# Block-causal attention with a gated MLP on one core: the value product of one pair moved directly ahead of the next pair's scores

## The chip, the core and the metric

The kernel runs on one core of one Trainium2 chip. The metric is the device time of one execution in microseconds (us). The kernel before the change has a median of 1179.65 us over three runs (1178.62 to 1180.1). PE is the matrix engine (TensorE), PEld its weight loads, DVE is VectorE, ACT is ScalarE, POOL is GpSimd, and SP is SyncE, whose queue issues most of the DMAs.

## What is computed

The reference, cut to what matters:

```python
# q, k, v: (B=8, H=8, S=576, D=64); block = 64
scores = (q @ k.T) / sqrt(D), masked to block_i >= block_j
attn   = exp(scores - max); attn = attn / (attn.sum(-1) + 1e-9)
x      = (attn @ v).transpose(0, 2, 1, 3).reshape(4608, 512)
gate   = 1 / (1 + exp(-(x @ w_gate)));  val = x @ w_val     # 512 -> 1536
out    = (gate * val) @ w_out                               # 1536 -> 512
```

Everything is float32 at the ends. Inside, many matrix products are made of three products of high and low parts (`H*H + H*L + L*H`), whose operands carry the letters H and L in the profile.

## The kernel before, in words

**Stages.** The 64 heads are taken as 32 pairs, four pairs for each of the 8 batches. A loop over `p` from 0 to 32 (lines 812 to 856) works on pair `p` and finishes pair `p-1` in the same turn. The first third of the MLP's hidden columns (`F1` = 4 blocks of 128) for batch `b` is computed while the attention of later batches runs; its matrix products are the filler between the attention's steps. After the loop the rest of that filler is run (lines 986 and 987), and then comes a second phase over the remaining hidden columns (`unit` and `out_block`, lines 887 to 977), which this change does not touch.

**One pair.** With rows of scores in 128-blocks `i` = 0 to 3 and a last block of 64 rows for both heads together (the tail):

- `s_blocks` (step `s`, line 393) makes the scores of blocks 3, 2 and (1, 0), each group in a PSUM tile of two banks. The two heads lie on partitions 0 to 63 and 64 to 127, and each has its own half of PE's rows (`tile_position=(64 * h, 0)`, line 377), so that two products run side by side. DVE writes the mask (lines 409, 411) and takes the row maximum (line 385), ACT takes exponentials into the tiles `P` (line 388).
- `s_tail` (step `t`, line 415) makes the tail's scores with the whole height of PE, six products of 288 columns; ACT writes the tile `Pt` (line 427).
- `tr_main(3)`, `tr_main(2)`, `tr_low`, `tr_tail` (steps `tr3`, `tr2`, `trl`, `trt`) transpose the exponentials on PE (line 262), and ACT copies them out of PSUM into `G1` and `G0` (line 363). The tail's copies go into columns of `G1` (line 485).
- `recip` (step `r`, line 430) turns the row sums into reciprocals, writes them to DRAM (`r_d`, line 439) and reads them back broadcast (`rb`, line 442), over SP's queue.
- `av` (step `AV`, line 493) multiplies with the values, 28 products in 14 side-by-side couples, where each head has its own half of PE's columns (`tile_position=(0, 64 * h)`, line 501). DVE multiplies the result by `rb` into `xT` (line 507). Then `finish` (line 512) casts `xT` on ACT, sends it to DRAM on ACT's queue and subtracts on POOL.
- `prep(p+1)` (steps `k` and `q`) transposes the next pair's K and Q on DVE (line 290), splits them on ACT, DVE and POOL (lines 327 to 336).

PE thus has three ways to be cut: the whole array (MLP products, the tail's scores, the transposes), two halves of rows (scores) and two halves of columns (AV).

**The order of the steps** stands in tuples of (step, places). `ALONE`, `FIRST` and `TURN` serve pairs 0 to 7, `REST` pairs 8 to 31. A place is a point behind a step at which MLP products are dealt out (lines 836 to 851): `rate` products for each place, which is 3.0 from pair 12 on, thus 36 for the 12 places of a pair. Step names in `REST` that begin with `AV` belong to pair `p-1`, the others to pair `p`. When the AV of a batch's last pair has been written down, the MLP products of that batch are added to those left, and `rate` is set anew so that 32 remain over when the next batch comes (lines 821 to 825). `k`, `q` and `r` have no place.

**What fixes the order on PE.** The program is scheduled by a list scheduler which simulates the engines; `behind(a, b)` (line 70) adds an edge that keeps `a` behind `b` without a semaphore. In the steps of `REST`:

- `hold` is the last matrix product of the latest scores or AV (lines 402 and 504). Every transpose and every product dealt out later stands behind it (lines 263, 845).
- `dealt` is the last MLP product dealt out. The first product of the scores (line 401) and of the AV (line 503) stands behind it.
- A product that is dealt out also stands behind the attention's step of three places earlier (`AHEAD` = 3, lines 847 and 848), so it may run up to three places early where the attention's step is not ready.

**PSUM.** The scores, the AV and the transposes of `REST` take their two-bank tiles (`two_banks`, line 267) from one rotation of three, in the order in which the steps are written down; MLP products use two further single banks (`mbank`).

Of the kernel before, what the change touches and what calls it, by code (L numbers as in the profile page):

```python
# [21 lines left out]
AHEAD = 3  # L22
# [8 lines left out]
         ("tr3", 1), ("r", 0), ("ld", 0))  # L31
ALONE = (("S3", 1), ("TR2", 1), ("k", 1), ("S2", 1), ("q", 1), ("m3", 0), ("m2", 0), ("TRt", 1), ("t", 1), ("TRl", 1), ("sl", 1), ("AV", 2),
         ("tr3", 1), ("r", 0), ("ld", 0))
REST = (("s", 3), ("t", 1), ("AV", 2), ("tr3", 1), ("r", 0), ("k", 0), ("tr2", 1), ("q", 0), ("trl", 2), ("trt", 2))
TURN = (("s3", 1), ("TR2", 1), ("k", 0), ("s2", 1), ("TRt", 1), ("q", 0), ("t", 1), ("TRl", 1), ("sl", 1), ("AV", 1),
        ("tr3", 1), ("r", 0), ("tr2", 1), ("trl", 1), ("trt", 1))
N_FIRST = 7
# [5 lines left out]
def attn_glu_kernel(ctx: ExitStack, tc: tile.TileContext, q, k, v, w_gate, w_val, w_out, out):  # L43
# [26 lines left out]
    def behind(ins, other):  # L70

        tc.add_manual_dep(ins, other.name, mybir.DependencyInfo(mybir.DependencyClass.NoSync,
                                                                mybir.DependencyReason.DATA), reason="order")
# [84 lines left out]
    def run(gen):  # L158
        for _ in gen:
            pass  # L160
# [3 lines left out]
    with ExitStack() as s2:  # L164
# [78 lines left out]
        pe_last, first_mm, hold, dealt, chain = [], [], [], [], []  # L243
# [23 lines left out]
        def two_banks():  # L267
            return ps_a.tile([P, 2, 512], F32, name="bank")
# [80 lines left out]
        def attend(p):  # L349
# [10 lines left out]
            rest = p > N_FIRST  # L360
# [4 lines left out]
            def scores(ps, i, c):  # L365


                n = P * (i + 1)
                q = slice(i * P, (i + 1) * P)
                ops = [(KQ[:, 1, q], KQ[:, 0, :n])]  # L370
                if rest and i:
                    q = slice((i - 1) * P, i * P)
                    ops = [(QS[a][:, q], KS[b][:, :n]) for a, b in ((0, 0), (1, 0), (0, 1))]
                for k, (x, y) in enumerate(ops):
                    for h in range(2):
                        matmul(ps[:, h, c:c + n], lhsT=x[rows(h)], rhs=y[rows(h)], start=(k == 0),
                               stop=(k == len(ops) - 1), tile_position=(64 * h, 0))
                        if h == k == 0:
                            first_mm[:] = pe_last

            def softmax(ps, i, c):
                n = P * (i + 1)
                c0 = col[i]
                Pi = keep[i] = p_tile(i)
                mark("DVE", nc.vector.tensor_reduce(out=nm[:, c0:c0 + 2], in_=ps[:, :, c:c + n], axis=AX.X, op=ALU.max,  # L385
                                                    negate=True))
                for h in range(2):
                    mark("ACT", nc.scalar.activation(out=Pi[:, h], in_=ps[:, h, c:c + n], func=AF.Exp,  # L388
                                                     bias=nm[:, c0 + h:c0 + h + 1], accum_out=sm[:, 5 * h + i:5 * h + i + 1]))
                    if i == 3 and 0 < p < NP:  # L390
                        behind(last["ACT"], q_copied[-1])

            def s_blocks(*groups, alone=False):


                tiles = [two_banks() for _ in groups]
                for k, (ps, group) in enumerate(zip(tiles, groups)):
                    for j, i in enumerate(group):
                        scores(ps, i, 2 * P * j)
                        if rest and dealt and k == j == 0:  # L400
                            behind(first_mm[0], dealt[-1])
                if rest:
                    hold[:] = pe_last
                if alone:
                    yield
                for ps, group in zip(tiles, groups):
                    n = P * (group[0] + 1)
                    if len(group) == 1:
                        nc.vector.memset(ps[0:64, :, n - 64:n], -1e9)  # L409
                    else:  # L410
                        nc.vector.memset(ps[0:64, :, P:3 * P].rearrange("p h (i n) -> p h i n", i=2)[:, :, :, 64:], -1e9)
                    for j, i in enumerate(group):
                        softmax(ps, i, 2 * P * j)
# [109 lines left out]
            def step(what):  # L523
                if what in ("S3", "S2"):
                    soft[what] = s_blocks((int(what[1]),), alone=True)
                    next(soft[what])
                elif what in ("m3", "m2"):
                    run(soft.pop("S" + what[1]))
                elif what == "s":
                    run(s_blocks((3,), (2,), (1, 0)))  # L530
                elif what[0] == "s":
                    run(s_blocks({"s3": (3,), "s2": (2,), "sl": (1, 0)}[what]))
                elif what == "t":
                    s_tail()
                elif what == "r":
                    recip()
                elif what == "tr3":
                    tr_main(3)
                elif what == "tr2":
                    tr_main(2)  # L540
                elif what == "trl":
                    tr_low()
                elif what == "trt":
                    tr_tail()
                else:
                    av()
                    finish()
# [243 lines left out]
        pe_ticks = []  # L791

        def convert_to(p, part):
            for j, plan in enumerate(CONV_PLAN):
                convert_until(j, sum(plan[i] for i in plan if i < p) + int(plan.get(p, 0) * part))
# [3 lines left out]
        def early_work(p, tick):  # L799

            when = p - (n - 1), tick
            if when in ((0, 0), (1, 0)):
                early.append(fetch_gv(0, 0, 0, len(early)))
                early_x.append(x_load(0, len(early_x)))
            if when == (0, TICKS - 2):
                sums_gv(*early[0], alone=last["DVE"])
            if when == (1, 1):
                x_sums(early_x[0], nc.vector, last["DVE"])
            if when == (1, 4):
                sums_gv(*early[1], alone=last["DVE"])  # L810

        for p in range(n + 1):
            early_work(p, 0)
            pr = prep(p + 1) if p + 1 < n else iter(())
            now = attend(p) if p < n else None
            tick = 0
            for what, places in (ALONE if p < NP else FIRST if p < N_FIRST else TURN if p == N_FIRST else REST):
                if what.startswith(("AV", "TR")):
                    if prev:
                        prev(what.lower() if what == "AV" else what.lower()[:2] + what[2:])  # L820
                    if prev and what == "AV" and pairs[p - 1][1] == NP - 1:
                        pb = pairs[p - 1][0]
                        mlp = itertools.chain(mlp, mlp1(pb, mbank if p < n else bank))
                        left += F1 * 6 * NC + 3 * F1 * 4
                        rate = (left - KEEP[pb > 0]) / (4 * TICKS)
                elif what in "kq":
                    next(pr, None)
                    if p >= NP and p + 3 < n:
                        load(p + 3, what)
                elif what == "ld":  # L830
                    if p < NP:
                        for x in "kq":
                            load(p + 3, x)
                elif now:
                    now(what)
                for _ in range(places if now else 6 if what == "AV" else 0):
                    pe_ticks.append(pe_last[0])
                    acc += rate
                    while acc >= 1:
                        acc -= 1  # L840
                        left -= 1
                        ins = next(mlp, None)
                        if ins is not None:
                            dealt[:] = [ins]
                            if hold:
                                behind(ins, hold[0])
                            if len(pe_ticks) > AHEAD:
                                behind(ins, pe_ticks[-1 - AHEAD])
                    tick += 1
                    convert_to(p, min(1.0, tick / (TICKS - 2)))  # L850
                    early_work(p, tick)
            convert_to(p, 1.0)
            run(pr)
            if 0 < p and p + 2 < n:
                load(p + 2, "v")
            prev = now
# [238 lines left out]
```

## Time and profile before

| | |
|---|---|
| median of three runs | 1179.65 us (1178.62 to 1180.1) |
| profiled execution, from its first to its last instruction (span) | 1177.6 us |
| DVE, ACT, POOL busy | 776.6, 617.4, 349.6 us |
| weight loads busy | 976.3 us |
| MLP products of 512 columns from `XH` on tile `m`, mean | 0.400 us |
| transposes of 128 columns on tile `bank`, mean | 0.273 us |

The profiled execution is listed with its span alone; what lies around the span is taken from the difference to the runs, 2.05 us to their median.

How to read it: a matrix product's row gives its modelled duration, which is longer than the distance to the next product, since products are pipelined. What a product costs is therefore read from the start of one row to the start of the next. In a timeline, neighbouring instructions of a kind are one row with a count (`x2` for the two halves side by side). The chain of work that ended last is listed as start, length and what ran. In a view by windows, each engine has its busy time in that stretch and its number of instructions in brackets.

### The profile page before, as it was taken

What the parts mean: (1) busy time and instruction counts of PE and PEld (TensorE: products, weight loads), DVE (VectorE), ACT (ScalarE), POOL (GpSimd) and SP (SyncE); (2) the same over time, 40 slices, a digit from 0 to 9 for tenths busy, and PEclk for the clock granted to TensorE, in tenths of its full rate; (3) what the DMA queues carried; (4) which work ended last, traced back from release to release, by engine and by line L of the source; (5) the groups of instructions that cost most, each with busy time, mean ns of one, the idle gap of its engine ahead of it and who ended that gap; (6) DMA issues with size and microseconds to landing.
All of it is one profiled execution on the core that took longest, in us unless ns stands there. A gap on an engine that the chain in (4) does not pass through costs nothing.

```text
span 1177.6 us, 19283 instructions
## 1 busy us (share of the span) xinstructions
PE 1153.6 (98%) x6749; PEld 976.3 (83%) x6749; DVE 776.6 (66%) x1405; ACT 617.4 (52%) x1364; POOL 349.6 (30%) x390
## 2 busy tenths in 40 slices
PE   6999999999999999999999999999999999999998
PEld 4555778778777877787889899999999998998997
DVE  5778845454564555457959977867877746746754
ACT  5867766766676676666334443553453422423421
POOL 2345523222331322234002133032033263262330
PEclk8999999999999999999999999999999999999999
DMA  8765434435434443534323236235197455164241
GB/s 198 180 144 115 104 89 100 117 74 127 99 89 112 102 122 71 125 105 134 111 95 126 91 120 223 71 136 202 39 339 276 158 172 179 39 212 132 83 143 54
DMA packets 253361, 153.34 MB, mean 130 GB/s; under 512 B 193232, under 2 KB 215248, under 8 KB 252624
## 3 DMA queue, kind: packets, MB, share of 16 engines
q1 hardware_dynamic: 241600, 132.15, 40.1%
q10 hardware_dynamic: 11280, 18.91, 4.4%
q8 instruction: 53, 0.87, 0.3%
q0 software_dynamic: 384, 1.05, 0.3%
q14 instruction: 44, 0.36, 0.1%
HBM read 104.73 MB, written 47.33 MB: 129 GB/s over the span
## 4 chain that ended last, share of the span: by engine, by line
PE 90%; DVE 5%; ACT 2%; issue 1%; DMA 1%; POOL 0%; SPq 0%; DVEq 0%; ACTq 0%
PE b L875 27%; PE bank L258 14%; PE m L131 14%; PE m L953 11%; PE m L138 7%; PE bank L262 6%; PE b L953 5%; PE bank L131 3%; ACT P L388 1%; PE m L262 1%; PE bank L138 1%; DVE nm L385 1%; DVE XL L765 0%; DMA raw<-in_moe_w_out_dram 0%; DMA rqk<-in_k_dram 0%
## 5 line engine op out<-in xcount | busy, mean ns | idle before, releaser
L875 PE MATMUL b<-XH,w 128*128 128x384 f32 x1344 | 349.2, 335 | 1.2 <-DVE g L921 1.2
L875 PEld LDWEIGHTS b<-XH,w 128*128 128x128 f32 x1344 | 243.9, 188 | 5.2 <-DVE g L921 1.6
L875 PE MATMUL b<-XL,w 128*128 128x384 f32 x672 | 223.5, 335 | 0.0
L388 ACT ACTIVATE P<-bank,nm 128x512 f32<-128x512 f32 (+3 forms) x256 | 132.1, 530 | 68.3 <-DVE nm L385 68.2
L385 DVE TENSOR_REDUCE nm<-bank 128x2 f32<-128x1024 f32 (+3 forms) x128 | 105.4, 823 | 40.7 <-ACT P L388 37.6
L875 PEld LDWEIGHTS b<-XL,w 128*128 128x128 f32 x672 | 126.1, 188 | 1.6
L953 PE MATMUL m<-wo,hH 128*128 128x512 f32 x384 | 125.0, 391 | 0.0
L363 ACT COPY G<-bank 128x768 f32<-128x768 f32 (+3 forms) x140 | 93.2, 694 | 26.2 <-PE bank L262 25.3
L258 PE MATMUL bank<-G,VS 128*64 128x320 f32 (+4 forms) x896 | 93.9, 360 | 0.1
L751 POOL TENSOR_TENSOR XB<-XB 128x384 f32<-128x384 f32 x20 | 20.7, 1037 | 237.9 <-DMA XB<-xT_d 191.6
L138 PE MATMUL m<-wo,hH 128*128 128x512 f32 x256 | 85.4, 398 | 1.4 <-ACT ost L632 1.0
L258 PEld LDWEIGHTS bank<-G,VS 128*64 128x64 f32 x896 | 55.9, 137 | 36.7 <-issue 4.3
L900 ACT ACTIVATE g<-g 128x384 f32<-128x384 f32 x72 | 37.8, 526 | 88.5 <-DVE g L913 48.6
L953 PEld LDWEIGHTS m<-wo,hH 128*128 128x128 f32 x384 | 72.0, 188 | 13.5
L131 PE MATMUL m<-XH,wv 128*128 128x512 f32 x240 | 82.3, 400 | 0.0
L131 PE MATMUL m<-XH,wg 128*128 128x512 f32 x240 | 82.1, 399 | 0.0
L764 ACT CAST XH<-XB 128x1536 fp32r<-128x1536 f32 (+2 forms) x72 | 65.2, 941 | 29.4 <-DVE XB L762 24.1
L765 DVE TENSOR_TENSOR XL<-XB,XH 128x1536 fp32r<-128x1536 f32 (+2 forms) x72 | 75.8, 1084 | 0.0
L262 PEld LDWEIGHTS bank<-ident,P 128*128 128x128 f32 x560 | 65.8, 141 | 11.5 <-ACT P L388 0.8
L953 PE MATMUL m<-wo,hL 128*128 128x512 f32 x192 | 75.2, 392 | 0.0
L262 PE MATMUL bank<-ident,P 128*128 128x128 f32 x560 | 74.8, 273 | 0.1
L409 DVE MEMSET bank<- 64x128 f32 x64 | 10.6, 165 | 88.0 <-PE bank L258 87.3
(183 smaller groups left out, 2339.5 us busy)
## 6 DMA issues: line engine op xcount, KB each, us to landing
xT_d<-xT ACTq DMA_DIRECT2D x32, 288.0 KB
XB<-xT_d SPq DMA_DIRECT2D x16, 576.0 KB
part_d<-ost SPq DMA_DIRECT2D x36, 256.0 KB
VS<-in_v_dram SPq DMA_DIRECT2D x64, 128.0 KB
part_d<-ost ACTq DMA_DIRECT2D x32, 256.0 KB
rqk<-in_k_dram SPq DMA_DIRECT2D x108, 72.0 KB
rqk<-in_q_dram SPq DMA_DIRECT2D x108, 72.0 KB
wgv_d<-st SPq DMA_DIRECT2D x8, 896.0 KB
```

Source lines behind the costliest of these rows:

```text
L131: mm = nc.tensor.matmul(ps, lhsT=lh, rhs=rh, start=(i == 0), stop=(i == n - 1))
L138: mm = nc.tensor.matmul(ps, lhsT=lh[:, f, t * P:(t + 1) * P], rhs=rh, start=(f == i == 0), stop=(f == F1 - 1 and i == 2))
L258: pe_last[:] = [nc.tensor.matmul(*args, **kw).ins]
L262: pe_last[:] = [nc.tensor.transpose(*args).ins]
L363: mark("ACT", nc.scalar.copy(out=dst, in_=src))
L385: mark("DVE", nc.vector.tensor_reduce(out=nm[:, c0:c0 + 2], in_=ps[:, :, c:c + n], axis=AX.X, op=ALU.max, negate=True))
L388: mark("ACT", nc.scalar.activation(out=Pi[:, h], in_=ps[:, h, c:c + n], func=AF.Exp, bias=nm[:, c0 + h:c0 + h + 1], accum_out=sm[:, 5 * h ...
L764: nc.scalar.copy(out=XO[j][0][:, a:b], in_=x)
L765: sub = nc.vector.tensor_sub(out=XO[j][1][:, a:b], in0=x, in1=XO[j][0][:, a:b].bitcast(F32))
L875: mm = nc.tensor.matmul(ps, lhsT=lh, rhs=rh, start=(first and k == 0), stop=(k == n - 1), skip_group_check=not first)
L900: mark2("ACT", nc.scalar.activation(out=t, in_=c, func=AF.Tanh, scale=0.5))
L953: mm = nc.tensor.matmul(po[t], lhsT=lh[:, f, t * P:(t + 1) * P], rhs=rh, start=(half == 0 and i == 0), stop=(half == 1 and i == 5))
```

## The change

Three things are changed, all for pairs 8 to 31, with one side effect on pair 7.

- In `REST` the step `AV` (of pair `p-1`) moves from behind the tail's scores to the front, ahead of the scores of pair `p`, and has no place. Its two places go to `s` (3 becomes 4) and to `t` (1 becomes 2). A pair has 12 places as before.
- The first product of the scores now stands behind both the last MLP product dealt out and `hold`, which at that point is the AV's last product; so the scores follow the AV.
- An MLP product that is dealt out behind `trt` stands behind the tail's transposes themselves (`ahead_by` = 0 in place of `AHEAD` = 3). In `REST` these are two places, six products at a rate of 3.0. The AV, next in order, stands behind the last of them. The step `trt` of `TURN` (pair 7, one place) falls under the same rule.

```diff
-REST = (("s", 3), ("t", 1), ("AV", 2), ("tr3", 1), ("r", 0), ("k", 0), ("tr2", 1), ("q", 0), ("trl", 2), ("trt", 2))
+REST = (("AV", 0), ("s", 4), ("t", 2), ("tr3", 1), ("r", 0), ("k", 0), ("tr2", 1), ("q", 0), ("trl", 2), ("trt", 2))
...
                         scores(ps, i, 2 * P * j)
-                        if rest and dealt and k == j == 0:
-                            behind(first_mm[0], dealt[-1])
+                        if rest and k == j == 0:
+                            for ins in (*dealt, *hold):
+                                behind(first_mm[0], ins)
...
                             if hold:
                                 behind(ins, hold[0])
-                            if len(pe_ticks) > AHEAD:
-                                behind(ins, pe_ticks[-1 - AHEAD])
+                            ahead_by = 0 if what == "trt" else AHEAD
+                            if len(pe_ticks) > ahead_by:
+                                behind(ins, pe_ticks[-1 - ahead_by])
```

Since the AV of a batch's last pair now comes four places earlier in the turn, the products of that batch are added four places earlier too. Counted through the loop, 976 products have been dealt out by the end of pair 31 where 964 had been before; the total is the same.

## Prediction

> **What bounds the kernel now.** First the page: the busy times and the chain that ended last.
>
> ```profile
> PE 1153.6 (98%) x6749; PEld 976.3 (83%) x6749; DVE 776.6 (66%) x1405; ACT 617.4 (52%) x1364; POOL 349.6 (30%) x390
> PE 90%; DVE 5%; ACT 2%; issue 1%; DMA 1%; POOL 0%; SPq 0%; DVEq 0%; ACTq 0%
> ```
>
> PE carries the chain. Second the view by windows, for the stage that the change edits (most of pairs 9 to 31 with their MLP filler) and for the rest of the filler. The columns are window, its length, busy time of PE, PEld, DVE, ACT, POOL with instruction counts, and the granted clock.
>
> ```profile
> 188.97:546.00 357.03, 357.03 (x2442) 282.86 (x2443) 194.78 (x383) 240.80 (x599) 100.58 (x142) 1.00 0.44 104
> 546.00:615.00 69.00, 69.00 (x316) 56.30 (x313) 52.20 (x90) 26.91 (x40) 8.77 (x5) 1.00 0.36 114
> ```
>
> PE is not idle for one moment of the first 357 us, at full clock. In such a stage only two things can move the time: PE's own work becomes shorter, or PE is made to wait where it does not wait now. No product is added or removed here, so a gain has to come from what products cost by their order. Third, then, the chain in order of time through one pair (start, length, what, count):
>
> ```profile
> 356.88 2.00 PE bank L258 x21
> ...
> 361.85 3.65 PE bank L258 x34
> 365.49 1.58 PE m L131 x6
> ...
> 372.49 0.55 PE bank L262 x5
> 373.04 0.92 PE m L131 x4
> 373.96 2.00 PE bank L258 x21
> ```
>
> A pair takes 373.96 - 356.88 = 17.08 us. The 21 are the scores, the 34 the tail's scores (6) and the AV (28), the five the tail's transposes, with four MLP products between them and the next scores.
>
> **What a change of PE's cut costs.** Fourth, the timeline of PE around these places. `x2` is a couple side by side.
>
> ```profile
> 356.25 0.63 PE L138 MATMUL m<-wo,hH 128*128 128x512 f32 x2
> 356.81 0.50 PE L258 MATMUL bank<-KH,QH 64*128 64x512 f32 x2
> 357.14 0.39 PE L258 MATMUL bank<-KH,QL 64*128 64x512 f32 x2
> 357.38 0.40 PE L258 MATMUL bank<-KL,QH 64*128 64x512 f32 x2
> ...
> 362.21 0.29 PE L258 MATMUL bank<-KH,QBL 128*128 128x288 f32 x1
> 362.34 0.29 PE L258 MATMUL bank<-KL,QBH 128*128 128x288 f32 x1
> 362.56 0.49 PE L258 MATMUL bank<-G,VS 128*64 128x320 f32 x2
> ...
> 364.89 0.60 PE L258 MATMUL bank<-G,VS 128*64 128x256 f32 x6
> 365.42 0.50 PE L131 MATMUL m<-XL,wg 128*128 128x512 f32 x1
> 365.75 0.39 PE L131 MATMUL m<-XH,wg 128*128 128x512 f32 x1
> ```
>
> The mean of the AV's widest form is in the groups by form:
>
> ```profile
> L258 PE MATMUL bank<-G,VS 128*64 128x320 f32 x384 | 58.7, 441 | 0.1
> ```
>
> An MLP product in a row of such takes 0.92 / 4 = 0.23 us (the x4 row of the chain). Against that:
>
> - MLP to scores: two products take 356.81 - 356.25 = 0.56, so the second 0.33; the first couple of scores 0.33; the next one, of the same 512 columns, 0.24. Two steps, each 0.10 too long: 0.20 us.
> - Tail's scores to AV: the last product takes 0.22 where the one before took 0.13, 0.09 too long. The first AV couple has a duration of 0.49 where the mean of its form is 0.44, 0.05 too long (an estimate, durations being modelled): 0.14 us.
> - AV to MLP: the last three couples (256, 128 and 128 columns) take 0.53. The whole AV takes 365.42 - 362.56 = 2.86 us for 3200 columns (each product of values and probabilities is two instructions); with the long steps off, some 2.71, so 512 columns should take 0.43: 0.10 too long. The first MLP product takes 0.33: 0.10 too long. Together 0.20 us.
> - Scores to MLP is left as it is by the change, and cancels.
>
> So each change of cut costs 0.14 to 0.20 us, in two steps. Fifth, the two crossings that the new order needs and that appear early in the trace, scores to AV in pair 1 and MLP to AV in pair 8, with tail's scores to MLP ahead of the latter:
>
> ```profile
> 42.55 0.60 PE L258 MATMUL bank<-KQ 64*128 64x256 f32 x6
> 43.08 0.49 PE L258 MATMUL bank<-G,VS 128*64 128x320 f32 x2
> ...
> 170.75 0.29 PE L258 MATMUL bank<-KL,QBH 128*128 128x288 f32 x1
> 170.88 0.40 PE L131 MATMUL m<-XH,wg 128*128 128x512 f32 x1
> 171.21 0.49 PE L258 MATMUL bank<-G,VS 128*64 128x320 f32 x2
> ```
>
> From row halves to column halves, three couples of the same 512 columns take 0.53 again, 0.10 too long, and the first AV couple has the same 0.49: 0.15 us. Two tiled steps next to each other thus pay as much as a tiled one next to the whole array. MLP to AV: 0.33 for 0.23, plus 0.05: 0.15 us. Tail's scores to MLP: 0.13, the ordinary distance: nothing.
>
> **The sum.** Before, a pair crosses MLP to scores (0.20), scores to MLP, tail to AV (0.14), AV to MLP (0.20). After, it crosses MLP to AV (0.15), AV to scores, scores to MLP, and the tail's scores lie between MLP products at no cost. AV to scores is not in the trace. Its lower bound is nothing, the upper one a full AV to MLP and a full MLP to scores, 0.40. I take 0.20, by the nearest row, scores to AV, which pays one crossing and not two; the scores' own second step is 0.10, the AV's last 0.10. The gain of a pair is 0.20 + 0.14 + 0.20 - 0.15 - 0.20 = 0.19 us. Over 24 pairs that is 4.6 us (with AV to scores at nothing 9.4, at 0.40 nothing or 0.2 lost).
>
> [...]
>
> **What could wait.** The held products cost PE nothing (transposes to MLP is crossed once, as now). They are the cover for the copies out of the tail's transposes, which the AV needs at once now, where scores and tail's scores lay between before. ACT's rows, and DVE's ahead of the mask:
>
> ```profile
> 364.97:373.82 8.85, 5.57 (x10) 1.00 0.54 124
> ```
>
> ```profile
> 367.81 0.68 ACT L514 CAST XH<-xT 128x576 fp32r<-128x576 f32 x1
> ...
> 373.07 0.75 ACT L363 COPY G<-bank 128x512 f32<-128x512 f32 x2 [1.60 <-PE bank L262]
> ```
>
> ```profile
> 357.94 0.17 DVE L409 MEMSET bank<- 64x128 f32 x1 [5.99 <-PE bank L258]
> ```
>
> The copies end at 373.82, 0.78 us after the transposes (373.04). Six products cover 6 x 0.23 = 1.38: 0.60 us to spare if ACT takes the copies at once. Without cover each pair would lose the 0.78, 19 us in all.
>
> ACT's queue is in order. The first row is ACT from the end of the exponentials to the end of these copies: 5.57 busy of 8.85 us, among it 0.68 for the cast of `xT`. After the change the AV starts 17.08 - 0.19 - 2.87 (3.65 less the tail's six at 0.13) = 14.02 after the scores, that is 370.90 on this scale, so 5.93 us behind the exponentials. The cast moves to the free time ahead of the next exponentials, and 4.89 us remain for those 5.93. It fits, with 1.04 us for waits inside. So I cost the wait at nothing.
>
> DVE's multiplication into `xT` comes ahead of the softmax, in its idle 5.99 us. It holds one of the three PSUM tiles, which the last group of scores now needs, two groups (about 1.3 us) after the AV's end; the two multiplications take 0.8. SP's queue keeps its order behind pair `p`'s reciprocals, and the loads of `VS`, which wait for AV, come earlier:
>
> ```profile
> 368.22 1.74 SPq L442 DMA_DIRECT2D rb<-r_d  x3
> ```
>
> ```profile
> 46.89 1.98 DMA VS<-in_v_dram
> ```
>
> The three issues end at 369.96; with some 2 us to landing (an estimate from the second row, a DMA on the chain) `rb` is there at 371.9, 15.1 after its scores. The first multiplication wants the AV's 2432 first columns of 3200, about 2.1 us behind the AV's start, 16.1 after the scores: 1.0 to spare.
>
> Pair 7's tail transposes have two held products behind them instead of six. Cover 0.46 to 0.6 for 0.78 and a weight load: up to 0.4 us once. I take 0.4.
>
> **Behind the loop.** Twelve products (2.7 us) come ahead of the last AV instead of behind it. PE's total stays, but the DVE work that starts with the last AV has 2.7 us less of PE's time beside it until
>
> ```profile
> 597.80 0.69 DVE L150 SCALAR_TENSOR_TENSOR h<-t,bank 128x512 f32<-128x512 f32 x1 [1.78 <-PE bank L131]
> ```
>
> where DVE waits for PE, for the first time since its block began. Bounds 0 and 2.7 - 1.78 = 0.9 us if the order is kept, 2.7 at most. I take nothing, since products of the last batch can fill in. From there on PE leads, and all moves up together.
>
> Together 4.6 - 0.4 = 4.2 us: span 1177.6 - 4.2 = 1173.4. The median of before lies 2.05 us above the span, so 1175.4 us. About 0.2% (2.4 us) is what a measurement of this kernel can tell from no change.
>
> **Rivals.**
>
> 1. *Slower: the AV waits for the tail's copies.* If ACT's order puts two further steps of 0.6 us (a glu's cast and tanh) between the transposes and the copies, the copies end 1.2 later, 0.6 past the cover; 24 x 0.6 = 14.4, less 4.2: 1190 us. It decides from 0.19 us past the cover for each pair, that is, when the copies start 0.8 us or more behind the transposes. For it: ACT is 4.89 of 5.93 us full there. Against: the copies are ready ahead of what the held products set free. 0.13.
> 2. *Part of it is lost* to the same wait in some pairs, or behind the loop: 1 to 3.5 us lost, 1176.4 to 1178.9. 0.15.
> 3. *The price moves along.* If AV to scores pays leaving and entering in full, four steps of 0.10, 0.40 in all, the gain of a pair is nothing: 1179.65, with pair 7's 0.4 1180. Against it: every crossing in the trace has two long steps. It also covers the case that the scheduler keeps MLP products between AV and scores. 0.10. [...]
>
> [...]
>
> 4. *More:* AV to scores is nearly free: 24 x 0.39 - 0.4 = 9.0, 1170.7. Against: scores to AV is not free. 0.07.
>
> The forecast, a gain of 3.3 to 5.3, has 0.55.
>
> **Numbers.** The range 1172.5 to 1180.5 takes in the forecast, rivals 2 and 3 and a little of the others; outside lie most of 1 and 4, under 0.2. Faster by over 0.2% (under 1177.3): forecast, 4 and two thirds of 2 (0.10), 0.72. Same: rival 3 and the rest of 2, 0.15. Slower: rival 1, 0.13.
>
> **What would show it.** Right: pairs from 12 on take 16.9 us in the chain, PE is still busy in all of that stage, the AV and the 21 scores stand as one row of about 4.9 us, the step from the AV's last couples to the scores is 0.53 again, and six MLP products stand between the tail's transposes and the AV. Wrong: PE waits on ACT's copies (line 363) or DVE's `xT` (line 507) at the AV or the scores; an AV-to-scores step that is not 0.1 long; a stretch from 546 to 615 with PE idle.

## The result, and the profile after

The kernel after takes 1192.81 us (median of four runs, 1190.52 to 1194.33); the kernel before, on the same chip, 1179.24 (four runs, 1178.62 to 1180.1). The ratio is 1.0111, with a 95% interval of 1.0099 to 1.0123: slower by 13.6 us, where 4.2 us less was forecast. The profiled execution has a span of 1190.0 us against 1177.6. Among all the runs below, one execution, of run 3, took 5636 us; it is left out of that run's figures.

The page of the kernel after, its busy times and the chain that ended last (line numbers are one higher than before from line 402 on, two higher from 849 on):

```profile
PE 1154.5 (97%) x6749; PEld 978.9 (82%) x6749; DVE 777.9 (65%) x1405; ACT 616.6 (52%) x1364; POOL 344.6 (29%) x390
PE 80%; DVE 7%; DMA 5%; SPq 3%; issue 3%; ACT 2%; POOL 0%; DVEq 0%; ACTq 0%
```

PE does the same work in about the same busy time, but carries 80% of the chain instead of 90%. DMA, DVE and SP's queue have come in. PE's waits from 164 to 546 us (total, times, longest), a stretch in which it had none:

```profile
PE bank L258 <- DVE xT L508: 6.0, 7, 1.6
```

The instruction that waits is the first product of the scores of blocks (1, 0). It needs the PSUM tile that the AV has just filled, and DVE frees that tile with the multiply into `xT`. What that multiply waited for stands in the view of the tile `rb`, from 164 to 546 us: total idle time of DVE ahead of the multiply, and in how many pairs.

```profile
L508 DVE TENSOR_TENSOR xT<-bank,rb x43: 414/491/492, 173.8 to 545.9; 128x320 f32<-128x320 f32 x22, 128x256 f32<-128x256 f32 x21
its engine sat idle before it (us, times) until:
  DMA rb<-r_d: 51.2, 11
  DMA rqk<-in_k_dram: 24.8, 6
  PE bank L258: 19.3, 4
  DMA rqk<-in_q_dram: 6.4, 1
```

In 18 of 22 pairs a DMA ended DVE's idle time, by this view `rb` itself or a load on the same queue, and only in 4 it was the AV. The same view of the kernel before has no idle time ahead of the multiply at all. The chain in order of time, here through one of the worst pairs, reads as a loop from one pair's tail's scores to the next pair's scores:

```profile
420.71 4.79 PE m L138 x20
425.50 0.81 PE bank L258 x6
426.33 0.77 DVE nm L426
427.12 0.84 ACT Pt L428 x2
...
428.69 0.30 SPq L440
...
430.54 0.50 SPq L239
...
432.76 0.60 SPq L443
...
433.39 4.17 DMA rb<-r_d
...
437.69 0.10 DVE xT L508
...
438.66 0.85 PE bank L258 x10
```

Twenty MLP products, the tail's scores (x6), maximum, exponential, reciprocals, the write of `r_d`, two loads of K, the read of `rb`, the multiply, and then the ten products of scores that had to wait. The timeline of PE shows the wait itself:

```profile
432.67 2.93 PE L258 MATMUL bank<-G,VS 128*64 128x320 f32 x28
...
436.68 0.34 PE L258 MATMUL bank<-KL,QH 64*128 64x384 f32 x2
438.66 0.39 PE L258 MATMUL bank<-KH,QH 64*128 64x256 f32 x2 [1.64 <-DVE xT L508]
```

The worst place is pair 8, whose moved AV belongs to pair 7: PE's waits there are

```profile
127.03 2.93 PE L258 MATMUL bank<-G,VS 128*64 128x320 f32 x28 [1.86 <-ACT G L363]
135.32 0.39 PE L258 MATMUL bank<-KH,QH 64*128 64x256 f32 x2 [3.95 <-DVE xT L508]
```

What was forecast for PE's cuts is there too: where no wait comes between, AV and scores stand as one row of some 4.9 us (50 products); the rows are under run 1.

### The profile page after: what moved, and what is told of

It is laid out like the page before. It is cut to its first block, busy times and chain, and to the rows that moved or that the text cites. A ratio compares the mean times of both kernels' runs of the same rounds, so it can differ in the third digit from the quotient of the medians.

```text
span 1190.0 us, 19165 instructions
## 1 busy us (share of the span) xinstructions
PE 1154.5 (97%) x6749; PEld 978.9 (82%) x6749; DVE 777.9 (65%) x1405; ACT 616.6 (52%) x1364; POOL 344.6 (29%) x390
## 4 chain that ended last, share of the span: by engine, by line
PE 80%; DVE 7%; DMA 5%; SPq 3%; issue 3%; ACT 2%; POOL 0%; DVEq 0%; ACTq 0%
PE b L877 27%; PE m L131 12%; PE m L955 11%; PE bank L258 10%; PE m L138 6%; PE b L955 5%; PE bank L262 4%; PE bank L131 3%; DMA rb<-r_d 2%; SPq L443 1%; ACT P L388 1%; SPq L440 1%; PE bank L138 1%; DMA rqk<-in_k_dram 1%; DMA r_d<-rT 1%
## 5 line engine op out<-in xcount | busy, mean ns | idle before, releaser
L508 DVE TENSOR_TENSOR xT<-bank,rb 128x320 f32<-128x320 f32 x64 | 26.4, 453 | 114.1 <-DMA rb<-r_d 56.8
L363 ACT COPY G<-bank 128x768 f32<-128x768 f32 (+3 forms) x140 | 90.2, 698 | 8.4 <-PE bank L262 7.6
L520 POOL TENSOR_TENSOR XL<-xT,XH 128x576 fp32r<-128x576 f32 x32 | 46.6, 1455 | 155.9 <-ACT XH L515 155.9
L515 ACT CAST XH<-xT 128x576 fp32r<-128x576 f32 x32 | 21.6, 674 | 109.9 <-DVE xT L508 109.9
```

The source lines that it names most:

```text
L363: mark("ACT", nc.scalar.copy(out=dst, in_=src))
L520: nc.gpsimd.tensor_sub(out=XL[:, hp], in0=xT, in1=XH[:, hp].bitcast(F32))
```

## The experiments

The theory: the crossings are saved as forecast, but the AV now needs the reciprocals' broadcast `rb` before it has landed. The late multiply holds the PSUM tile, and the scores of blocks (1, 0) wait for that. Rivals: ACT's copies of the tail's transposes; the six held products; crossings that save nothing. Medians of before differ a little from chip to chip (1178.66, 1178.99 and 1179.2 us under the runs below), so each result has its ratio.

### 1 and 2: no reciprocals in the multiply, after and before

```diff
-in0=pv[:, i, :n], in1=rb[:, q0:q0 + n]
+in0=pv[:, i, :n], in1=one[:, q0:q0 + n]
```

The tile `one` is filled once with ones; in both runs `rb`, which nothing reads any more, has one buffer instead of two.

> The changed kernel, whose xT multiply reads a tile of ones instead of the reciprocals' tile rb (the softmax is left unnormalized; the reciprocals and their DMAs are still issued, and nothing reads them). Every engine's order stays that of the changed kernel. Theory (the moved AV's PSUM tile is held until the reciprocals land, and the scores of blocks 1 and 0 wait for that tile): the stalls at line 258 behind DVE's xT go, pairs come back to some 16.9 us each, and the time falls from 1192.8 to 1175 to 1177 us; a wait of some 1.9 us for ACT's copies at the first moved AV stays. Rival 1 (ACT's copies of the tail, or the held products, are what costs): 1190 us or more, as the changed kernel. Rival 2 (the shorter crossing saves nothing): 1179 us, the kernel before.

> The kernel before with the same edit (softmax left unnormalized, the reciprocals' DMAs still issued). Theory: there the reciprocals land 6 us and more ahead of the AV, so nothing changes: 1179 us within 1.5. Rival (the multiply or its DMA costs something wherever the AV stands): some us less than 1179, and then the fall of the changed kernel is no evidence for the moved AV. The difference between this run and the changed kernel with the same edit is the price of the crossings alone: by the prediction 4.6 us.

After: 1172.8 us, ratio 0.9945 (0.9929 to 0.996) against 1178.66 of the unchanged kernel before. Before: 1178.55, ratio 0.9996 (0.9987 to 1.0005). The whole loss of the change hangs on the wait for `rb`: without it the change gains 5.75 us over the same kernel before, and before the change the reciprocals cost nothing. In its trace PE, DVE and ACT run their instructions in the same order as in the kernel after. The chain of the run after, by its rows of AV and scores, 18 pairs apart:

```profile
221.03 4.85 PE bank L260 x50
...
524.75 4.88 PE bank L260 x50
```

A pair takes 303.72 / 18 = 16.87 us, 0.21 less than the 17.08 of before. The crossing from AV to scores, which no trace of before had, is in the timeline of this run:

```profile
341.40 0.60 PE L260 MATMUL bank<-G,VS 128*64 128x256 f32 x6
341.93 0.50 PE L260 MATMUL bank<-KH,QH 64*128 64x512 f32 x2
342.27 0.40 PE L260 MATMUL bank<-KH,QL 64*128 64x512 f32 x2
342.51 0.39 PE L260 MATMUL bank<-KL,QH 64*128 64x512 f32 x2
```

The AV's last three couples take 0.53 again, and the first couple of scores 0.34 where the next takes 0.24: two steps, each 0.10 too long, the 0.20 us that the prediction took. The same two places of the chain in the kernel after:

```profile
225.93 5.09 PE bank L258 x50
...
542.57 4.29 PE bank L258 x40
```

So the kernel after is 4.9 us behind at the first and 17.8 at the second. At the AV of pair 6 it had been 0.4 us ahead (118.42 against 118.82), so 5.3 us are lost around pair 8 and 12.9 in the 18 pairs. Together with the 0.4 that is the difference of the two spans, 1190.0 - 1172.3 = 17.7; the medians lie 20.0 apart.

### 3 and 4: the suspected way made longer, after and before

```diff
+r_d2 = dram.tile([9, P], F32, name="r_d2", bufs=2)
+nc.sync.dma_start(out=r_d2, in_=r_d)
-r_f = r_d.rearrange("c q -> (c q)")
+r_f = r_d2.rearrange("c q -> (c q)")
```

> The changed kernel with one more DRAM-to-DRAM copy of 4.6 KB in the reciprocals' way (r_d to r_d2, then to rb): the landing comes some 2 us later in each of 24 pairs. Theory: each pair waits longer by most of it, 24 times 1 to 2 us: 1192.8 + 24 to 48 = 1217 to 1241 us. Rival (the reciprocals are not what the scores wait for, ACT's copies or the late tail are): 1193 us within 3.

> The kernel before with the same extra copy. Theory: the reciprocals had 6 us and more to spare there, so 2 us later costs nothing: 1179 us within 2. Rival (each added DMA on SP's queue or its transfer costs by itself): as much more than 1179 as the changed kernel with the copy is above 1192.8.

After: 1260.04 us (median of three runs), ratio 1.0697 (1.0676 to 1.0719), 67 us more than the kernel after and above what the theory gave. Its waits for `xT`:

```profile
PE bank L258 <- DVE xT L510: 50.1, 22, 5.8
```

The rest is partly PE's clock, whose mean is 0.969 here and 0.996 in the kernel after (profiled executions).

Before: 1186.2, ratio 1.0057 (1.0042 to 1.0072), where nothing was expected. The windows of this run tell where: columns as in the prediction.

```profile
0.00:123.00 123.00, 103.87 (x608) 66.53 (x609) 84.69 (x162) 82.58 (x223) 45.71 (x59) 0.93 0.62 149
...
164.00:546.00 382.00, 382.00 (x2606) 303.29 (x2605) 201.08 (x398) 255.84 (x637) 105.87 (x150) 1.00 0.43 104
```

In the first 123 us PE starts 608 matrix instructions where the kernel before has 656; from 164 to 546 us it is never idle and has 2606 of them, as many as before. So in the pairs that the change edits, the extra copy was free in the old order. The pairs of the first 123 us stand in another order of steps, and the copy was added there too: the miss was in taking all pairs alike. The granted clock is lower there as well, 0.93 where the kernel before has 0.96 in the same stretch. By this run at most some 7.5 of the 67 us above come from those pairs.

### 5: the tile freed without the reciprocals

```diff
-nc.vector.tensor_mul(out=xT[...], in0=pv[...], in1=rb[...])
+nc.vector.tensor_copy(out=xT[...], in_=pv[...])
...
+nc.gpsimd.tensor_mul(out=xT, in0=xT, in1=rb)
 cut = nc.scalar.copy(out=XH[:, hp], in_=xT)
```

This holds for pairs 8 to 31; the lower two lines run behind the tail's scores of the next pair (for pair 31 at once). Pairs up to 7 multiply as before.

> The changed kernel, in which DVE only copies the AV's tile to xT, and the multiply by rb runs later on GpSimd, SBUF to SBUF, with the rounding behind it; the result is the same. The reciprocals are used as before, but the PSUM tile no longer waits for them. Theory (it is the tile, held for rb, that the scores of blocks 1 and 0 wait for): the time of the run without the reciprocals, 1172.8, plus at most 3 for the added GpSimd work and for ACT's rounding: 1172 to 1176 us, below both kernels. Rival (the wait only moves, to ACT, whose in-order queue then stands behind the late multiply): 1180 us or more, with PE behind ACT's exponentials or copies.

1184.14 us, ratio 1.0038 (1.0023 to 1.0053): 8.7 us of the loss come back, not all, and the time lies outside the theory's range and inside the rival's. PE's waits for `xT` in the whole run, its waits for ACT's copies from 164 to 546 us in the second fence, and ACT's largest wait in the third:

```profile
PE bank L258 <- DVE xT L511: 4.0, 1, 4.0
```

```profile
PE bank L258 <- ACT G L363: 2.0, 4, 0.6
```

```profile
ACT XH L520 <- POOL xT L518: 121.6, 23, 6.5
```

The wait for `xT` is gone from 164 us on; the 4.0 is pair 7's, which the edit left as it was. Part of the rival holds as well: ACT, in order, now stands behind GpSimd's multiply, and in four pairs its copies of `G` come late. The run is 11.3 us above run 1. Of these, pair 7 makes up 8.0, by run 9 below, and the late copies 2.0. So from pair 9 on the tile was what the scores waited for; the expectation had overlooked pair 7.

### 6 and 7: the reciprocals sooner, in two ways

The first edit holds the loads of K (and of Q, which stood there already) behind the read of `rb`; in its trace PE, DVE, ACT and GpSimd run their instructions in the same order as in the kernel after. The second deals the places so that 12 products stand ahead of the tail's scores instead of 20.

```diff
+dma = queue.dma_start(...)
+if rb_dma:
+    behind(dma.ins, rb_dma[0])
```

```diff
-REST = (("AV", 0), ("s", 4), ("t", 2), ("tr3", 1), ...
+REST = (("AV", 0), ("s", 1), ("t", 5), ("tr3", 1), ...
```

> The changed kernel with the four loads of k held behind the reciprocals' DMAs on SP's queue; the order of PE, DVE, ACT and GpSimd stays as it was, instruction by instruction. Theory (the reciprocals land too late, and part of their 7 to 9 us is spent behind the loads of k): the landing comes 1 to 2 us earlier, most waits of 0.3 to 1.6 us go, the one of 4 us shrinks: 1177 to 1185 us. Rival (the loads cost nothing, the two hops take their time by themselves): 1192 us; a time over 1195 would say that k then comes too late.

> The changed kernel with the products' places dealt so that the tail's scores stand behind 12 MLP products instead of 20, as in the kernel before (places 1 and 5 instead of 4 and 2); the AV stays directly ahead of the scores and six products stay behind the tail's transposes. Theory (the chain from the tail's scores to rb started 8 products, 1.9 us, later than before the change): rb lands 1 to 1.9 us earlier and 1176 to 1185 us come out. Rival (the lateness of the tail's scores is no part of it): 1192 us; 1172.8 would say that it is all of it.

K behind `rb`: 1182.47, ratio 1.0022 (1.0012 to 1.0032). Tail's scores sooner: 1180.3, ratio 1.0011 (1.0002 to 1.0021). Both as the theory had it. The view of `rb` in the second run, same stretch, by its first row:

```profile
  PE bank L258: 85.2, 19
```

Now the AV ends DVE's idle time in 19 of 22 pairs, where it was 4. One wait of PE for `xT` is left, that of pair 8:

```profile
PE bank L258 <- DVE xT L508: 3.6, 1, 3.6
```

### 8 and 10: one part of the change alone

Run 8 is the kernel after with `ahead_by = AHEAD` always; run 10 the kernel before with `ahead_by = 0` at `trt`, and nothing else.

> The changed kernel without the second part: the AV stands ahead of the scores, but no product is held behind the tail's transposes, so the AV follows these directly. Theory (both parts belong together; rb's lateness comes from the AV's place): the AV now waits for the copies of the tail's transposes, 1 to 2 us in each of 24 pairs, which at the same time gives rb that time: 1205 to 1240 us, with PE's waits at the AV on ACT or DVE copies of G. Rival (the six held products are what made the change slower): 1175 to 1182 us.

> The kernel before with the second part alone: six products behind the tail's transposes, the AV where it was. Theory: the number of changes of PE's cut stays, no wait is added: 1179 us within 1.5. Rival (holding products behind the transposes costs by itself, as the transposes then stand closer together and wait for ACT's copies): 1183 us or more.

The AV alone: 1195.43, ratio 1.0137 (1.0122 to 1.0152). The held products alone: 1179.05, ratio 0.9999 (0.999 to 1.0008). The held products are not what cost. Without them the AV waits in each pair, as its timeline shows (one row of twenty like it):

```profile
333.07 2.93 PE L258 MATMUL bank<-G,VS 128*64 128x320 f32 x28 [0.68 <-ACT G L363]
```

That is 0.68 us, less than the 1 to 2 expected of this run, so that the time stayed below its range; the prediction's 0.78 without cover was nearer. It also delays the scores, so that `rb` is mostly there in time: the list of PE's waits has `xT` three times instead of eight.

### 9, 11 and 12: pair 8 in the old order, alone and with the rest

```diff
+REST8 = (("s", 3), ("t", 1), ("AV", 2), ("tr3", 1), ...
-... TURN if p == N_FIRST else REST
+... TURN if p == N_FIRST else REST8 if p == N_FIRST + 1 else REST
```

> The changed kernel in which pair 8 alone keeps the order of before (scores, tail's scores, then the AV of pair 7); from pair 9 on the AV stands ahead. Theory: the waits at the first moved AV (1.9 us for ACT's copies, then 4.0 us at the scores of blocks 1 and 0 for rb of pair 7) go, with the clock that they cost, and nothing else changes: 1192.8 less 5 to 7, so 1186 to 1188 us. Rival (the debt only moves to pair 9, as all pairs behind it have late reciprocals too): 1191 to 1193 us.

> The run with the tail's scores behind 12 products (1180.3 us; its profile still has 3.6 us behind xT and 1.9 us behind ACT's copies at the first moved AV, and no other wait for xT) and pair 8 in the order of before. Theory: these 5.5 us go, and what is left is the kernel without the wait for the reciprocals: 1173 to 1176 us, faster than both kernels. Rival (the wait comes back one pair later): 1179 to 1181 us.

> The same with the loads of k behind the reciprocals' DMAs. Theory: rb lands another 1 us earlier; where no wait for it is left this gains nothing, so the run before it within 1 us, 1172 to 1176; rival (rb's landing still sets part of the time in waits too short to be listed): 1 to 3 us below the run before it.

Pair 8 alone: 1184.82, ratio 1.0052 (1.0037 to 1.0067), 8.0 us better than the kernel after, where 5 to 7 were expected. With the tail's scores sooner: 1174.28, ratio 0.9961 (0.9949 to 0.9974). With K behind `rb` as well: 1174.61, ratio 0.9958 (0.9946 to 0.9971), so no further gain. Run 11 beats both kernels, with the whole softmax in it. Its view of `rb`:

```profile
  PE bank L259: 91.4, 21
  DMA rqk<-in_q_dram: 3.6, 1
```

## Why the prediction was wrong

**The step that failed** is the one in "What could wait" that puts `rb`'s landing at 15.1 us after its scores and its use at 16.1, "1.0 to spare". It was costed at nothing and was no rival. On the same scale, the pair above has its scores, its tail's scores and SP's issues at

```profile
417.44 0.50 PE L258 MATMUL bank<-KH,QH 64*128 64x512 f32 x2
```

```profile
419.86 0.39 PE L258 MATMUL bank<-KH,QH 64*128 64x256 f32 x2 [0.93 <-DVE xT L508]
...
425.34 0.29 PE L258 MATMUL bank<-KH,QBH 128*128 128x288 f32 x1
```

```profile
428.69 1.37 SPq L440 DMA_DIRECT2D r_d<-rT  x4
430.16 0.87 SPq L239 DMA_DIRECT2D rqk<-in_k_dram  x2
431.21 2.79 SPq L443 DMA_DIRECT2D rb<-r_d  x3
```

- The issues end at 434.00, 16.6 after the scores; the prediction had 13.1, read off the old order. The tail's scores start 7.9 us after the scores, where the prediction's rows of before have 5.0 (361.85 - 356.88). Eight more MLP products (1.9 us) stand ahead of them, because the AV's two places went to `s` and `t`, as the text on the change says, and 0.93 us of this pair's own scores was waiting, which delays the next AV as well. The prediction moved the AV and left the tail's scores where they were.
- From the last issue to the landing (433.39 + 4.17 = 437.56) it takes 3.6 us; the prediction took 2, from a load of `VS` at another place. Landing is thus at 20.1 instead of 15.1.
- The use was misjudged too, the other way. The prediction let the first multiply start 2.1 us behind the AV's start. In run 1, where it waits for the AV alone, it starts 3.0 behind it, when the whole AV is done:

```profile
339.07 2.93 PE L260 MATMUL bank<-G,VS 128*64 128x320 f32 x28
```

```profile
342.08 0.82 DVE L510 TENSOR_TENSOR xT<-bank,one 128x320 f32<-128x320 f32 x2 [3.93 <-PE bank L260]
```

The AV at 432.67 starts 15.2 after the scores, so the use is at 18.2, and `rb` is 1.9 late in place of 1.0 to spare. Little of that is hidden: from the row at 436.68 to the one at 438.66 PE needs 1.98 us where run 1 needs 0.17.

This pair is one of the worst. The landing can be read from the trace in each pair, as the last semaphore update of the three reads. For the pairs between 190 and 545 us its medians, counted from the pair's scores, are:

| | landing | use |
|---|---|---|
| prediction | 15.1 | 16.1 |
| kernel before | 16.4 | 17.0, had only the AV moved (14.0 + 3.0) |
| run 1, where nothing waits for it | 17.3 | 17.0 |
| kernel after | 17.7 (16.7 to 20.9) | 17.0, later by the pair's own wait |
| run 7, tail's scores sooner | 16.2 | 17.0 |

So the 1.0 to spare would have been some 0.6 with the tail's scores at their old place, and the eight products made it 0.3 too late in the median pair, more in others. The multiplies bear it out: of the 21 between 190 and 545 us, run 1 and run 7 each start all but one no later than 3.0 us behind their AV's start, and the kernel after starts 16 later than that.

Runs 6 and 7 show that an earlier landing by either way brings back more than half of the 20 us between the kernel after and run 1: 10.3 us by the queue, 12.5 by the eight products. The prediction did name a wait for `xT` among the signs of being wrong, but gave it no price and no chance. That rival 1 came out at 1190 us, near the 1192.8 measured, is luck: its wait, for ACT's copies, is absent from pair 9 on.

**Pair 7** was given 0.4 us. Its AV waited 1.86 for ACT's copies and its scores 3.95 for `rb`; run 9 measures the place at 8.0, the clock behind these waits included. In the old order this AV stood behind two more steps, which hid both.

**The forecast's own mechanism was right.** A pair without the wait takes 16.87, 0.21 us less (0.19 forecast); run 1 gains 5.75 us over run 2 (4.6 forecast, and the runs' intervals reach 1.8 and 1.1 us to either side). The crossing from AV to scores costs the 0.20 us that were taken for it, as the rows under run 1 show, so rival 3, a price that moves along, is out. That the six products were a sufficient cover is shown by the kernel after, which has no wait for ACT's copies from 164 us on; run 8 gives what they cover, 0.68 us in a pair. Rival 1 named a mechanism that exists, but in the kernel after only at pair 8.

**Behind the loop** no loss shows: the pairs of run 1 gain 24 x 0.21 = 5.0 us, and the whole run 5.75. Pair 7's wait for the copies, 1.86 us, is in run 1 too, but other waits of the kernel before are gone there: from 123 to 164 us PE is idle for 2.07 us in run 1 and 1.83 before.

**Where the 12.9 us of the 18 pairs went.** The listed waits sum to 6.0 only. Added up from the start of one row to the next, against run 1, the step ahead of the first product of scores (1, 0) is 8.4 us longer in all, the scores behind it 2.1 and the twenty MLP products 2.4. A wait costs more than its listing, since a row's modelled duration reaches past the next start: 1.98 - 0.17 = 1.81 for the listed 1.64 above. Fifteen of the 18 pairs pay it, most of them some tenths of a microsecond. The MLP products' 2.4 is the clock (below), in two pairs.

That 12.5 and 8.0 us, found in runs 7 and 9, sum to 20.5 and run 11 brings 18.5 is within the intervals. What stays open is why some waits bring half the clock and others don't.

## What to carry to other kernels

When a step is moved earlier, list every input that it reads and trace each back to its start in the new order; a landing time that was read in the old order is not valid there, above all where the same edit hands out filler anew. A margin of 1 us that rests on estimates is a rival with a price, not a zero. A side input that takes a way over DRAM (here nine rows of reciprocals, landing at 17.7 us after the scores in the median pair, where the use was due at 17.0) can be the latest of all, and it then blocks not its own step but whoever needs the PSUM tile next. To price a suspected wait, feed the consumer a constant in both kernels: two runs separated the gain (5.75 us) from the loss (20 us) here.

## What the runs showed of the hardware

A short wait of PE can cost twice. In the chain of the kernel after, the 20 products behind the scores took 4.79 us where the wait had been 0.93 (the row at 420.71 above). Behind the waits of 1.64 us, and of 1.63 at

```profile
494.20 0.44 PE L258 MATMUL bank<-KH,QH 64*128 64x256 f32 x2 [1.63 <-DVE xT L508]
```

they took 6.37 and 5.85:

```profile
439.51 6.37 PE m L131 x20
...
495.49 5.85 PE m L138 x20
```

The granted clock (the column ahead of the DMA share) behind the waits of 0.93, 1.64 and 1.63 us:

```profile
419.86:425.50 5.64, 5.64 (x32) 4.68 (x33) 3.77 (x7) 4.81 (x16) 1.43 (x1) 1.00 0.49 119
439.85:443.24 3.39, 3.39 (x10) 2.65 (x9) 2.19 (x5) 3.19 (x11) 0.94 (x1) 0.51 0.45 131
494.45:497.80 3.35, 3.35 (x16) 2.64 (x15) 3.13 (x5) 2.52 (x8) 1.42 (x1) 0.50 0.78 202
```

Behind the two long waits the clock was at half for 3.4 us each, and 20 products took 1.58 and 1.06 us longer; behind the wait of 3.95 us at pair 8 there is a third such stretch (0.50 from 136.0 to 139.4 us). It isn't so each time: run 9 has waits of 1.82 and 1.66 us, and its clock stays at 1.00 in the window around both:

```profile
413.59 0.39 PE L259 MATMUL bank<-KH,QH 64*128 64x256 f32 x2 [1.82 <-DVE xT L509]
...
432.36 0.39 PE L259 MATMUL bank<-KH,QH 64*128 64x256 f32 x2 [1.66 <-DVE xT L509]
```

```profile
410.00:440.00 30.00, 26.53 (x182) 21.35 (x179) 14.93 (x28) 17.89 (x49) 5.20 (x8) 1.00 0.57 118
```

Why the clock was halved behind some waits and not behind others, no run here shows.

The landing of `rb` depended on what was issued ahead of it: holding four loads of K behind `rb`, with no other engine's order changed, brought the median landing from 17.7 to 17.1 us after the scores and gave back 10.3 us. In the pair above, `rb` took 3.6 us on SP's queue from its last issue to its landing, and in the median pair 2.9; in run 6, without the loads of K between, 2.5. A bound taken from one other DMA, the 2 us of the prediction, was too low here.
